# A decode step of attention and MLP on one core: K and V loaded with one key head to 32 partitions, and the softmax laid out to match

## The chip, the core and the metric

The kernel runs on one NeuronCore of one Trainium2 chip. The metric is device time in microseconds (us) of one execution; lower is better. Three runs of the kernel before gave 98.59, 98.72 and 98.76 us, so the median is 98.72 us. The profile was taken in a further execution, which took 98.62 us.

## What is computed

One token `x` of 1024 values goes through a layer norm. An attention block and an MLP work beside each other on the result, and both are added to `x`:

```python
xn = layernorm(x)
q = xn @ wq                                  # 32 query heads of 128; 4 key heads, 8 queries each
k, v = the last 4096 rows of each key head's cache
p = softmax(q k / sqrt(128));  o = p v       # per query head
A = o @ wo                                   # (1, 4096) @ (4096, 1024)
B = gelu(layernorm(xn) @ w1 + b1) @ w2 + b2  # 1024 -> 3584 -> 1024
out = x + A + B
```

Everything is bf16. Each weight and each cache row is read once: wq, wo 8.4 MB each, w1, w2 7.3 MB each, and of K and V 4.2 MB each (four key heads of 1 MB). That makes 39.86 MB from HBM for a few matrix rows of work.

## The kernel before

There is no planner: each engine's list is written out by hand, and semaphores tie the lists together. The order of the transfers is the order of SP's list, since one queue on SP issues nearly all of them.

**Transfers (SP).** wq in two pieces (L232, issued on L159), K in two (L230), w1 in one (L235). Then SP waits for turned K (L311) and loads V in two pieces into the same tile `KV` (L312). After the q projection (L313) it loads w2 in two pieces (L314) over wq's part of the tile `BIG`; after the first MLP product (`done["h"]`, L315) it loads wo in four pieces (L319) over w1's part and beyond. Line 159 is the helper's issue of every weight but wo.

**Layout of K and V.** `pairs` (L226) takes two key heads for one transfer: partition 2m+g holds 64 consecutive rows of head g, a run of 16 KB, so that each transfer of 2 MB covers all 128 partitions. Every partition holds rows of one head of each pair, and even and odd partitions hold different heads.

**Turning and scores.** VectorE turns K in 32x32 blocks of bf16, 128x4096 at a time, four times (`turn_k`, L284). q is turned the same way (L292) and spread into the zeroed tile `QBD` by four copies on VectorE and four on ScalarE (L303, L305). TensorE makes the scores in four PSUM banks: 32 matmuls of 128x512 (L467). Since two heads share the block of a turn, a first matmul per bank (L441) writes -1e30 where query and key head do not belong together.

**Softmax.** VectorE takes the maximum over 4 banks (L333) and over four groups of partitions (L337 to L342); ScalarE takes the exponential of 2048 columns (L345); VectorE turns the result into `PT` (L349). TensorE multiplies it with V in 32 matmuls (L496). The sum over partitions is a matmul with `B64` (L484); VectorE scales by the reciprocal with a mask `HALF` (L380) and adds the blocks.

**The MLP.** w1 is multiplied in 56 matmuls (L480), the gelu runs on small tiles (L358 to L371), and w2 and 16 of the 32 rows of wo go through 11 rounds of eight matmuls (L505). Each round waits for a count on `s_feed`, which GpSimd raises when transfers land (L407 to L414). The other 16 rows of wo come last (L530, L528), then two copies and the store (L401, L403).

All additions onto banks that are prepared beforehand go through one helper, so their matmuls carry its line, L424; they are told apart by their tiles.

Of the kernel before, what the change touches and what calls it, by code (L numbers as in the profile page):

```python
# [27 lines left out]
PAIRS = 2  # L28
FAR = -1e30
# [24 lines left out]
def bass_parallel_sum__sliding_block_cached__mixer_channel_mlp__decode_kernel(  # L54
# [22 lines left out]
    s_x, s_b1, s_b2, s_v, s_out = (nc.alloc_semaphore(n) for n in ("s_x", "s_b1", "s_b2", "s_v", "s_out"))  # L77
    s_w1 = sems("s_w1", len(W1_CHUNKS))
    s_wq = [nc.alloc_semaphore("s_wq")] * len(WQ_CHUNKS)
    s_k = sems("s_k", PAIRS)  # L80
# [19 lines left out]
    B64 = sb("B64", [128, 64], f32)  # L100
    HALF4 = sb("HALF4", [64, 4], f32)
    HALF = sb("HALF", [64, PAIRS], f32)
    OTHER = sb("OTHER", [2, 128], bf16)
    ALT = sb("ALT", [2, 512], bf16)
# [11 lines left out]
    QBD = sb("QBD", [128, PAIRS * 512], bf16)  # L116
    HT = sb("HT", [128, FC], f32)
    U2 = sb("U2", [128, FC], f32)
    MX2 = sb("MX2", [128, 2], f32)
    MX8 = sb("MX8", [32, 8], f32)  # L120
    MXR = sb("MXR", [32, 1], f32)
# [7 lines left out]
    REC = sb("REC", [64, 1], f32)  # L129
# [40 lines left out]
    def pool_wait():  # L170
# [15 lines left out]
    POOL.mark(pool.memset(HALF4[:, :], 1.0))  # L186
    POOL.mark(pool.memset(OTHER[:, :], FAR))
    POOL.mark(pool.memset(ALT[:, :], 0.0))
# [12 lines left out]
    POOL.mark(pool.affine_select(  # L201
        out=OTHER[:, :].rearrange("p (x g h) -> p x g h", g=2, h=REP),
        in_=OTHER[:, :].rearrange("p (x g h) -> p x g h", g=2, h=REP),
        pattern=[[0, 8], [-1, 2], [0, REP]], compare_op=ALU.not_equal, fill=0.0, base=0, channel_multiplier=1))
    POOL.mark(pool.affine_select(
        out=ALT[:, :].rearrange("p (x g) -> p x g", g=2), in_=ALT[:, :].rearrange("p (x g) -> p x g", g=2),
        pattern=[[0, 256], [-1, 2]], compare_op=ALU.not_equal, fill=1.0, base=0, channel_multiplier=1))
    POOL.mark(pool.affine_select(
        out=HALF4[:, :], in_=HALF4[:, :], pattern=[[-16, 4]], compare_op=ALU.is_ge, fill=0.0,
        base=0, channel_multiplier=1))  # L210
    pool_wait()
    POOL.mark(pool.affine_select(
        out=HALF4[:, :], in_=HALF4[:, :], pattern=[[16, 4]], compare_op=ALU.is_ge, fill=0.0,
        base=15, channel_multiplier=-1))
# [11 lines left out]
    def pairs(cache, c):  # L226
        return cache[0, 2 * c:2 * c + 2, SK - W:SK, :].rearrange("g (m i) d -> m g (i d)", m=64)

    def load_k(c):
        sp.dma_start(KV[:, c * 8192:(c + 1) * 8192], pairs(A_k_cache, c)).then_inc(s_k[c], 16)  # L230
# [9 lines left out]
    def layernorm_stats(src, n, name):  # L240
# [37 lines left out]
        out=B64[:, :].rearrange("p (k r) -> p k r", k=2),  # L278
        in_=identf[:, :].rearrange("p (q r) -> p r q", q=4).unsqueeze(1).to_broadcast([128, 2, 32, 4]),
# [12 lines left out]
    C["qtb"] = DVE.mark(dve.transpose(QTB, Q32))  # L292
# [3 lines left out]
    QD = QBD[:, :].rearrange("p (c e b h) -> p c e b h", c=PAIRS, e=4, b=4)  # L296
    QS = QTB.rearrange("p (j e c) -> p e c j", j=4, e=4)
    for b in range(4):
        for c in range(PAIRS):
            to = QD[32 * b:32 * b + 32, c, :, b, 16 * c:16 * c + 16].rearrange("p e (u j) -> p e u j", j=4)  # L300
            of = QS[32 * b:32 * b + 32, :, 4 * c:4 * c + 4, :]
            if PAIRS * b + c < 4:
                C["d_QBD"] = DVE.mark(dve.tensor_copy(to, of))  # L303
            else:
                C["a_QBD"] = ACT.mark(act.activation(out=to, in_=of, func=ACTF.Copy))  # L305
# [3 lines left out]
    V = KV[:, :]  # L309
    for c in range(PAIRS):  # L310
        sp.wait_ge(DVE.sem, C["kt", 2 * c + 1])  # L311
        sp.dma_start(V[:, c * 8192:(c + 1) * 8192], pairs(A_v_cache, c)).then_inc(s_v, 16)  # L312
    sp.wait_ge(done["q"], 8)  # L313
    load_chunks(W2, w2_p, W2_CHUNKS, D, s_w2)  # L314
    sp.wait_ge(done["h"], 7)  # L315
    c0 = 0
    for j, n in enumerate(WO_CHUNKS):
        first = (FC + c0) * D
        sp.dma_start(BIG[:, first:first + n * D], wo_flat[:, c0 * D:(c0 + n) * D]).then_inc(s_wo[j] if j else s_feed, HALF_FEED)  # L319
        c0 += n  # L320
# [9 lines left out]
    S = PS[:, 3 * 512:7 * 512]  # L330
    for n in range(2):
        dve.wait_ge(done["sc"], 3 + n)
        C["mx"] = DVE.mark(dve.tensor_reduce(  # L333
            out=MX2[:, n:n + 1], in_=S[:, 1024 * n:1024 * n + 1024], axis=AX.X, op=ALU.max))
    dve_wait()
    for b in range(4):
        DVE.mark(dve.tensor_copy(MX8[:, 2 * b:2 * b + 2], MX2[32 * b:32 * b + 32, :]))  # L337
    dve_wait()
    DVE.mark(dve.tensor_reduce(out=MXR[:, :], in_=MX8[:, :], axis=AX.X, op=ALU.max))
    dve_wait()  # L340
    for b in range(4):
        C["nmb"] = DVE.mark(dve.tensor_scalar(  # L342
            out=NMB[32 * b:32 * b + 32, :], in0=MXR[:, :], scalar1=-SCALE, scalar2=None, op0=ALU.mult))
# [14 lines left out]
    DVE.mark(dve.tensor_tensor(out=U2[:, :], in0=HT[:, :], in1=HT[:, :], op=ALU.mult))  # L358
    dve_wait()
    DVE.mark(dve.tensor_scalar(out=U2[:, :], in0=U2[:, :], scalar1=0.044715, scalar2=1.0,  # L360
                               op0=ALU.mult, op1=ALU.add))
    dve_wait()
    C["d_T"] = DVE.mark(dve.tensor_tensor(out=U2[:, :], in0=U2[:, :], in1=HT[:, :], op=ALU.mult))
# [11 lines left out]
    DVE.mark(dve.reciprocal(out=REC[:, :], in_=PS[0:64, 3 * 512:3 * 512 + 1]))  # L375
    dve_wait()
    dve.wait_ge(done["pv"], 8)
    for i in range(2):
        rows = slice(32 * i, 32 * i + 32)
        DVE.mark(dve.scalar_tensor_tensor(  # L380
            out=ONM.rearrange("p (i c d) -> p i c d", i=2, c=PAIRS)[:, i],
            in0=PS[rows, 512:1024].rearrange("p (c i d) -> p i c d", c=PAIRS, i=2)[:, i], scalar=REC[rows, 0:1],
            in1=HALF[rows, :].unsqueeze(2).to_broadcast([32, PAIRS, DH]), op0=ALU.mult, op1=ALU.mult))
    dve_wait()
    DVE.mark(dve.tensor_reduce(
        out=ON[:, :], in_=ONM.rearrange("p (g d) -> p d g", g=4), axis=AX.X, op=ALU.add))
# [30 lines left out]
    pe.reg_mov(turn, C["kt", 0])  # L417
# [39 lines left out]
    pe.wait_ge(DVE.sem, C["d_QBD"])  # L457
    K4 = KT[:, :].rearrange("p (x k) -> p x k", k=128)
    with pe.Fori(0, PAIRS) as c:
        pe.wait_ge(ACT.sem, C["a_QBD"])  # L460
        with pe.Fori(0, 2) as i:
            pe.wait_ge(DVE.sem, turn)
            pe.reg_add(turn, turn, 1)
            for n in range(2):
                for j in range(2):
                    for u in range(2):
                        last = add(PS[:, bass.ds(i * 1024 + (3 + n) * 512, 512)],  # L467
                                   QBD[:, bass.ds(c * 512 + (j * 256 + u * 128), 128)],
                                   K4[:, bass.ds(c * 64 + i * 32 + 16 * n, 16), j * 64 + 32 * u:j * 64 + 32 * u + 32])
            last.then_inc(done["sc"], 1)  # L470
        pe.reg_add(turn, turn, C["kt", 2] - C["kt", 1] - 1)
# [12 lines left out]
    pe.matmul(PS[0:64, 3 * 512:3 * 512 + 1], lhsT=B64[:, :], rhs=SUMP[:, :]).then_inc(done["tot"], 1)  # L484
    pe.wait_ge(ACT.sem, C["a_h8"])
    for c in range(4):
        last = add(turned[:, c], H8[:, c:512:4], FLIP[:, 0:7])
        if c == 0:
            pe.wait_ge(s_v, 32)
# [3 lines left out]
    V3 = V.rearrange("p (c x) -> p c x", c=PAIRS)  # L493
    with pe.Fori(0, 8) as i:
        for u in range(4):
            last = add(bank(1), PT[:, bass.ds(i * 256 + u * 64, 128)], V3[:, :, bass.ds(i * 1024 + u * 256, 256)])  # L496
        last.then_inc(done["pv"], 1)

    pe.wait_ge(DVE.sem, C["d_GT"])
    with pe.Fori(0, ROUNDS) as t:  # L500
        pe.wait_ge(s_feed, turn)
        pe.reg_add(turn, turn, 2 * HALF_FEED)
        for u in range(ROUND):
            for a in range(2):
                add(bank(7), GO[:, bass.ds(t * STEP + (LEAD + 2 * u - ROW - a), 128)],  # L505
                    BIG[:, bass.ds(t * (ROUND * D) + (u * D + a * 512), 512)])
# [8 lines left out]
    for j, n in enumerate(WO_ROWS[WO_HEAD:]):  # L515
# [6 lines left out]
        for c in range(c0, c0 + n):  # L522
            rhs = BIG[:, (FC + c) * D:(FC + c + 1) * D]
# [39 lines left out]
```

## Time and profile before

| | |
|---|---|
| median of three runs | 98.72 us |
| profiled execution | 98.62 us |
| its span on the core | 97.2 us (1.4 us lie around it) |
| read from HBM | 39.86 MB, 410 GB/s over the span |
| PE / DVE / ACT / POOL busy | 79.4 / 39.0 / 11.2 / 9.9 us |
| granted TensorE clock | 1.00 throughout |

A page of the profile shows busy time by engine, the span in 40 slices, the DMA queues, the chain of work that ended last, the costliest groups of instructions, and the transfers with the median time from issue to landing. PE is TensorE, DVE is VectorE, ACT ScalarE, POOL GpSimd; SPq is SP's list of transfers. A busy TensorE is not a TensorE at its peak. Idle time of an engine that does not set the end costs nothing. A transfer's time to landing includes the time it stands in its queue behind earlier ones; its own share is read from the landing of the one before it.

### The profile page before, as it was taken

How to read it: one execution, taken by the hardware profiler on the slowest of the kernel's cores; microseconds unless marked ns; L12 is line 12 of the kernel's file. 1: busy time of each engine (PE TensorE's matmuls, PEld its weight loads, DVE VectorE, ACT ScalarE, POOL GpSimd, SP SyncE). 2: the span in 40 equal slices, each digit the busy share in tenths (PEclk: the TensorE clock that was granted, in tenths of full speed). 3: DMA queues.
4: the chain of work that ended last, by engine and by line, in shares of the span. 5: the costliest groups of instructions: out<-in, count | busy, mean ns of one | idle time of the engine just before them, and what ended most of it. 6: DMA issues, size and time to landing. Idle time of an engine off the chain costs nothing.

```text
span 97.2 us, 1412 instructions
## 1 busy us (share of the span) xinstructions
PE 79.4 (82%) x389; PEld 33.4 (34%) x400; DVE 39.0 (40%) x54; ACT 11.2 (12%) x20; POOL 9.9 (10%) x27
## 2 busy tenths in 40 slices
PE   0000899977999999999299999899999999979982
PEld 0000134423444432343134444333334344334451
DVE  0000589840079986999945450060029000000001
ACT  0870000060000006000003500200000100000001
POOL 6999400000000000000000000000000000000000
DMA  2998888899999988889999999999899999899990
GB/s 64 651 473 378 378 378 378 378 458 432 401 431 549 590 378 378 378 378 401 415 431 431 431 492 431 431 458 394 384 475 499 458 431 431 368 389 436 388 379 3
DMA packets 1989, 39.88 MB, mean 410 GB/s; under 512 B 322, under 2 KB 324, under 8 KB 452
## 3 DMA queue, kind: packets, MB, share of 16 engines
q1 hardware_dynamic: 1876, 39.85, 95.7%
q10 hardware_dynamic: 112, 0.01, 0.1%
q8 instruction: 1, 0.02, 0.1%
HBM read 39.86 MB, written 0.00 MB: 410 GB/s over the span
## 4 chain that ended last, share of the span: by engine, by line
DMA 54%; PE 30%; DVE 11%; issue 1%; SPq 1%; ACT 1%
DMA BIG<-in_A_wo_dram 32%; PE PS L424 30%; DMA BIG<-in_A_wq_dram 22%; DVE KT L284 9%; SPq L319 1%; DVE Pb L292 1%; DVE QBD L303 1%; ACT Pb L290 1%; DVE Pb L401 0%; SPq L159 0%; PE PS L510 0%
## 5 line engine op out<-in xcount | busy, mean ns | idle before, releaser
L424 PE MATMUL PS<-BIG,GO 128*128 (+1 forms) x137 | 21.5, 334 | 1.8 <-POOLq L414 0.8
L284 DVE STREAM_TRANSPOSE KT<-KV 128x4096 bf16<-128x4096 bf16 x4 | 17.5, 4424 | 6.9 <-DMA KV<-in_A_k_cache_dram 6.9
L424 PE MATMUL PS<-BIG,XZ 128*128 x64 | 14.0, 379 | 1.3 <-DMA BIG<-in_A_wq_dram 1.3
L424 PEld LDWEIGHTS PS<-BIG,GO 128*128 (+1 forms) x148 | 9.9, 97 | 13.5 <-issue 5.9
L424 PE MATMUL PS<-BIG,YZ 128*128 x56 | 12.4, 380 | 0.1
L428 PE MATMUL PS<-QBD 128*128 128x512 bf16 x38 | 10.1, 434 | 0.4 <-POOL HALF L217 0.4
L424 PEld LDWEIGHTS PS<-BIG,XZ 128*128 x64 | 6.2, 97 | 9.0 <-issue 2.7
L424 PE MATMUL PS<-KT,QBD 128*128 x32 | 7.4, 380 | 1.9 <-DVE KT L284 1.9
L420 PE MATMUL PS<-XBRP,onesb 1*128 1x512 bf16 x2 | 1.0, 617 | 9.7 <-DMA XBRP<-in_A_x_dram 9.7
L424 PE MATMUL PS<-KV,KT 128*128 x32 | 8.3, 381 | 0.5
L401 DVE CAST Pb<-PS 64x256 bf16<-64x256 f32 x1 | 0.4, 416 | 20.0 <-PE PS L510 20.0
L424 PEld LDWEIGHTS PS<-BIG,YZ 128*128 x56 | 5.4, 96 | 7.1 <-issue 1.2
L428 PEld LDWEIGHTS PS<-QBD 128*128 128x128 bf16 x38 | 4.0, 108 | 6.9 <-issue 3.7
L242 DVE BATCH_NORM_STATS2 BN<-PS 128x6 f32<-128x512 f32 x2 | 1.3, 688 | 10.7 <-PE PS L420 10.7
L424 PEld LDWEIGHTS PS<-KT,QBD 128*128 x32 | 3.0, 97 | 6.2 <-issue 3.3
L424 PEld LDWEIGHTS PS<-KV,KT 128*128 x32 | 3.1, 96 | 5.3 <-issue 3.8
L380 DVE SCALAR_TENSOR_TENSOR QBD<-PS,REC,HALF 32x256 f32<-32x256 f32 x2 | 0.9, 474 | 6.8 <-PE PS L424 6.8
L345 ACT ACTIVATE Pb<-PS,NMB 128x2048 bf16<-128x2048 f32 x1 | 2.0, 1967 | 13.8 <-DVE NMB L342 13.8
L420 PEld LDWEIGHTS PS<-XBRP,onesb 1*128 1x128 bf16 x2 | 0.1, 108 | 9.7 <-DMA XBRP<-in_A_x_dram 9.7
L349 DVE STREAM_TRANSPOSE KT<-Pb 128x2048 bf16<-128x2048 bf16 x1 | 2.3, 2310 | 2.1 <-ACT Pb L345 2.1
L333 DVE TENSOR_REDUCE MX<-PS 128x1 f32<-128x1024 f32 x2 | 2.4, 1206 | 1.3 <-PE PS L424 1.3
L354 DVE COPY HT<-PS 128x28 f32<-128x28 f32 x1 | 0.2, 207 | 6.2 <-PE PS L424 6.2
(81 smaller groups left out, 42.1 us busy)
## 6 DMA issues: line engine op xcount, KB each, us to landing
BIG<-in_A_wq_dram SPq DMA_DIRECT2D x1, 7168.0 KB, 21.1
BIG<-in_B_w_dram SPq DMA_DIRECT2D x1, 7168.0 KB, 46.0
KV<-in_A_k_cache_dram SPq DMA_DIRECT2D x2, 2048.0 KB, 27.7
KV<-in_A_v_cache_dram SPq DMA_DIRECT2D x2, 2048.0 KB, 14.5
BIG<-in_B_w_dram SPq DMA_DIRECT2D x1, 4096.0 KB, 20.5
BIG<-in_A_wo_dram SPq DMA_DIRECT2D x1, 4096.0 KB, 23.1
BIG<-in_B_w_dram SPq DMA_DIRECT2D x1, 3072.0 KB, 27.1
BIG<-in_A_wo_dram SPq DMA_DIRECT2D x1, 2816.0 KB, 29.4
```

Of the source, the lines that this page charges most:

```text
L242: DVE.mark(dve.bn_stats(out=BN[:, 12 * n + 6 * i:12 * n + 6 * i + 6], in_=src[:, 512 * i:512 * i + 512]))
L284: C["kt", n] = DVE.mark(dve.transpose(KT[:, n * 4096:(n + 1) * 4096], KV[:, n * 4096:(n + 1) * 4096]))
L290: C["q32"] = ACT.mark(act.activation(out=Q32, in_=bank(7), func=ACTF.Copy))
L292: C["qtb"] = DVE.mark(dve.transpose(QTB, Q32))
L303: C["d_QBD"] = DVE.mark(dve.tensor_copy(to, of))
L319: sp.dma_start(BIG[:, first:first + n * D], wo_flat[:, c0 * D:(c0 + n) * D]).then_inc(s_wo[j] if j else s_feed, HALF_FEED)
L333: C["mx"] = DVE.mark(dve.tensor_reduce(out=MX2[:, n:n + 1], in_=S[:, 1024 * n:1024 * n + 1024], axis=AX.X, op=ALU.max))
L345: C["exp"] = ACT.mark(act.activation(out=Pb[:, :], in_=S, func=ACTF.Exp, bias=NMB[:, 0:1], scale=SCALE, accum_out=SUMP[:, 0:1]))
L349: C["d_pt"] = DVE.mark(dve.transpose(PT[:, 0:2048], Pb[:, :]))
L420: last = pe.matmul(bank(2 + i), lhsT=onesb[0:1, :], rhs=XB[0:1, 8 * i:8 * i + 8, :])
L424: return pe.matmul(to, lhsT=lhsT, rhs=rhs, start=False, stop=False, skip_group_check=True, **place)
L428: pe.matmul(to, lhsT=zeros[:, 0:128], rhs=zeros[:, 0:512], skip_group_check=True, **how)
```

## The change

- **Layout.** K and V are each loaded by four transfers of 1 MB. Head g goes to partitions 32g to 32g+31, each of which holds 128 consecutive rows, a run of 32 KB. K's four transfers share one semaphore, and so do V's.
- **Place of V.** V no longer goes over K, but over wq's part of `BIG`. SP issues it right after the q projection, and no longer waits for K to be turned. The second piece of w2 and the first of wo now lie in w1's part and wait for `done["h"]`; the last three pieces of wo lie over V and wait for `done["pv"]`.
- **Turning.** K, q and the exponentials are turned as 32-bit words that hold two bf16 values, so each turn has half the elements.
- **Scores.** 32 matmuls as before, into two banks instead of four. `QBD` becomes a sliding window, and no -1e30 mask is written: four matmuls with zeros take the place of the masks. GpSimd no longer builds `OTHER`, `ALT` and `HALF`, and zeroes a tile `PT` of 128x4096 (over K) once K is turned.
- **Softmax.** One maximum over 1024 columns; the maximum over groups of partitions by two 128x32 turns and a reduction; the exponential of 1024 columns; four turns of 32 partitions into `PT`. In both kernels the maximum is one value per query head; the scaling (four instructions of 32x128) needs no mask any more.
- **Gelu.** Two instructions in place of three ahead of the exponential.

The core of the diff:

```diff
-    def pairs(cache, c):
-        return cache[0, 2 * c:2 * c + 2, SK - W:SK, :].rearrange("g (m i) d -> m g (i d)", m=64)
-    def load_k(c):
-        sp.dma_start(KV[:, c * 8192:(c + 1) * 8192], pairs(A_k_cache, c)).then_inc(s_k[c], 16)
+    def load_cache(dst, cache, semaphore):
+        for g in range(HKV):
+            sp.dma_start(dst[32 * g:32 * g + 32, :], cache[0, g, SK - W:SK, :].rearrange("(m i) d -> m (i d)", m=32)).then_inc(
+                semaphore, 16)
...
     def turn_k(n):
-        dve.wait_ge(s_k[n // 2], 16)
-        C["kt", n] = DVE.mark(dve.transpose(KT[:, n * 4096:(n + 1) * 4096], KV[:, n * 4096:(n + 1) * 4096]))
+        if n == 0:
+            dve.wait_ge(s_k, 16 * HKV)
+        C["kt", n] = DVE.mark(dve.transpose(
+            KT[:, n * 4096:(n + 1) * 4096].bitcast(f32), KV[:, n * 4096:(n + 1) * 4096].bitcast(f32)))
...
-    for c in range(PAIRS):
-        sp.wait_ge(DVE.sem, C["kt", 2 * c + 1])
-        sp.dma_start(V[:, c * 8192:(c + 1) * 8192], pairs(A_v_cache, c)).then_inc(s_v, 16)
     sp.wait_ge(done["q"], 8)
-    load_chunks(W2, w2_p, W2_CHUNKS, D, s_w2)
+    load_cache(V, A_v_cache, s_v)
+    load_chunks(W2, w2_p, W2_CHUNKS[:1], D, s_w2)
     sp.wait_ge(done["h"], 7)
+    load_chunks(W2, w2_p, W2_CHUNKS[1:], D, s_w2[1:], W2_CHUNKS[0])
     for j, n in enumerate(WO_CHUNKS):
-        first = (FC + c0) * D
+        first = (c0 - TAIL if j else TAIL + FC) * D
+        if j == 1:
+            sp.wait_ge(done["pv"], 8)
...
+    pool.wait_ge(DVE.sem, C["kt", 3])
+    C["PT"] = POOL.mark(pool.memset(PT, 0.0))
...
     C["exp"] = ACT.mark(act.activation(
-        out=Pb[:, :], in_=S, func=ACTF.Exp, bias=NMB[:, 0:1], scale=SCALE, accum_out=SUMP[:, 0:1]))
+        out=Pb[:, 0:1024].rearrange("p (x s w) -> p x w s", s=32, w=2),
+        in_=S.rearrange("p (x w s) -> p x w s", s=32, w=2),
+        func=ACTF.Exp, bias=NMB[:, 0:1], scale=SCALE, accum_out=SUMP[:, 0:1]))
+    dve.wait_ge(POOL.sem, C["PT"])
     dve.wait_ge(ACT.sem, C["exp"])
-    C["d_pt"] = DVE.mark(dve.transpose(PT[:, 0:2048], Pb[:, :]))
+    for g in range(HKV):
+        rows = slice(32 * g, 32 * g + 32)
+        C["d_pt"] = DVE.mark(dve.transpose(
+            PT[rows, :].bitcast(f32).rearrange("p (x a g h) -> p x a g h", a=4, g=HKV, h=REP)[:, :, :, g, :],
+            Pb[rows, 0:1024].bitcast(f32)))
...
-        pe.matmul(PS[:, bass.ds(n * 512 + 3 * 512, 512)], lhsT=OTHER[:, :], rhs=ALT[:, :], start=True, stop=False,
+        pe.matmul(PS[:, bass.ds(n * 512 + 3 * 512, 512)], lhsT=GO[:, 0:128], rhs=GO[:, 0:512], start=True, stop=False,
...
-        for u in range(4):
-            last = add(bank(1), PT[:, bass.ds(i * 256 + u * 64, 128)], V3[:, :, bass.ds(i * 1024 + u * 256, 256)])
+        for u in range(2):
+            for w in range(2):
+                last = add(bank(1), PT[:, bass.ds(i * 512 + (u * 256 + w), 128, step=2)],
+                           V[:, bass.ds(i * 2048 + (u * 1024 + w * 512), 512)])
```

More of the change, by code (lines that the diff above doesn't have):

```diff
@@ L99, in bass_parallel_sum__sliding_block_cached__mixer_channel_mlp__decode_kernel @@
     E4 = sb("E4", [32, 4 * 128], bf16)
[L100 to L104, printed above, removed]
+    B128 = sb("B128", [128, 128], f32)
     EDGE = sb("EDGE", [2, 132], bf16)
@@ L185, in bass_parallel_sum__sliding_block_cached__mixer_channel_mlp__decode_kernel @@
     POOL.mark(pool.memset(EDGE[:, :], 0.0))
[L186 to L188 removed]
+    POOL.mark(pool.memset(MX[:, 0:32], 0.0))
     POOL.mark(pool.memset(E4[:, :], 0.0))
@@ L291, in bass_parallel_sum__sliding_block_cached__mixer_channel_mlp__decode_kernel @@
     dve.wait_ge(ACT.sem, C["q32"])
-    C["qtb"] = DVE.mark(dve.transpose(QTB, Q32))
+    C["qtb"] = DVE.mark(dve.transpose(QTB.bitcast(f32), Q32.bitcast(f32)))
     dve_wait()
@@ L295, in bass_parallel_sum__sliding_block_cached__mixer_channel_mlp__decode_kernel @@
     act.wait_ge(POOL.sem, C["consts"])
-    QD = QBD[:, :].rearrange("p (c e b h) -> p c e b h", c=PAIRS, e=4, b=4)
-    QS = QTB.rearrange("p (j e c) -> p e c j", j=4, e=4)
-    for b in range(4):
-        for c in range(PAIRS):
[L300 to L305, printed above, removed]
+    QD = QBD[:, 0:4 * QW].rearrange("p (w n e) -> p w n e", w=2, e=2)
+    QS = QTB.rearrange("p (j e c w) -> p w c j e", j=4, e=2, w=2)
+    for g in range(HKV):
+        rows = slice(32 * g, 32 * g + 32)
+        to = QD[rows, :, 24 + 32 * g:32 + 32 * g, :].rearrange("p w (u j) e -> p w u j e", j=4)
+        of = QS[rows, :, 2 * g:2 * g + 2, :, :]
+        if g < 2:
+            C["d_QBD"] = DVE.mark(dve.tensor_copy(to, of))
+        else:
+            C["a_QBD"] = ACT.mark(act.activation(out=to, in_=of, func=ACTF.Copy))
     for n in range(2, 4):
         turn_k(n)
-    V = KV[:, :]
-    for c in range(PAIRS):
-        sp.wait_ge(DVE.sem, C["kt", 2 * c + 1])
-        sp.dma_start(V[:, c * 8192:(c + 1) * 8192], pairs(A_v_cache, c)).then_inc(s_v, 16)
     sp.wait_ge(done["q"], 8)
-    load_chunks(W2, w2_p, W2_CHUNKS, D, s_w2)
+    load_cache(V, A_v_cache, s_v)
+    load_chunks(W2, w2_p, W2_CHUNKS[:1], D, s_w2)
     sp.wait_ge(done["h"], 7)
+    load_chunks(W2, w2_p, W2_CHUNKS[1:], D, s_w2[1:], W2_CHUNKS[0])
     c0 = 0
     for j, n in enumerate(WO_CHUNKS):
-        first = (FC + c0) * D
+        first = (c0 - TAIL if j else TAIL + FC) * D
+        if j == 1:
+            sp.wait_ge(done["pv"], 8)
         sp.dma_start(BIG[:, first:first + n * D], wo_flat[:, c0 * D:(c0 + n) * D]).then_inc(s_wo[j] if j else s_feed, HALF_FEED)
@@ L328, in rows_of @@
         return values.rearrange("p (r u) -> p r u", u=ROUND).unsqueeze(2).to_broadcast([128, n, 2, ROUND])
[L330 to L334, printed above, removed]
+    pool.wait_ge(DVE.sem, C["kt", 3])
+    C["PT"] = POOL.mark(pool.memset(PT, 0.0))
+    S = PS[:, 3 * 512:5 * 512]
+    dve.wait_ge(done["sc"], 4)
+    DVE.mark(dve.tensor_reduce(out=MX[:, 0:1], in_=S, axis=AX.X, op=ALU.max))
     dve_wait()
-    for b in range(4):
-        DVE.mark(dve.tensor_copy(MX8[:, 2 * b:2 * b + 2], MX2[32 * b:32 * b + 32, :]))
+    DVE.mark(dve.transpose(MX[:, 32:64], MX[:, 0:32]))
     dve_wait()
-    DVE.mark(dve.tensor_reduce(out=MXR[:, :], in_=MX8[:, :], axis=AX.X, op=ALU.max))
+    DVE.mark(dve.tensor_reduce(
+        out=MX[:, 64:96].rearrange("p (a h) -> p a h", a=4),
+        in_=MX[:, 32:64].rearrange("p (a h) -> p h a", a=4).unsqueeze(1).to_broadcast([128, 4, REP, 4]),
+        axis=AX.X, op=ALU.max))
     dve_wait()
-    for b in range(4):
-        C["nmb"] = DVE.mark(dve.tensor_scalar(
-            out=NMB[32 * b:32 * b + 32, :], in0=MXR[:, :], scalar1=-SCALE, scalar2=None, op0=ALU.mult))
+    DVE.mark(dve.transpose(MX[:, 96:128], MX[:, 64:96]))
+    dve_wait()
+    C["nmb"] = DVE.mark(dve.tensor_scalar(out=NMB[:, :], in0=MX[:, 96:97], scalar1=-SCALE, scalar2=None, op0=ALU.mult))
     act.wait_ge(DVE.sem, C["nmb"])
     C["exp"] = ACT.mark(act.activation(
-        out=Pb[:, :], in_=S, func=ACTF.Exp, bias=NMB[:, 0:1], scale=SCALE, accum_out=SUMP[:, 0:1]))
+        out=Pb[:, 0:1024].rearrange("p (x s w) -> p x w s", s=32, w=2),
+        in_=S.rearrange("p (x w s) -> p x w s", s=32, w=2),
+        func=ACTF.Exp, bias=NMB[:, 0:1], scale=SCALE, accum_out=SUMP[:, 0:1]))
+    dve.wait_ge(POOL.sem, C["PT"])
     dve.wait_ge(ACT.sem, C["exp"])
-    C["d_pt"] = DVE.mark(dve.transpose(PT[:, 0:2048], Pb[:, :]))
+    for g in range(HKV):
+        rows = slice(32 * g, 32 * g + 32)
+        C["d_pt"] = DVE.mark(dve.transpose(
+            PT[rows, :].bitcast(f32).rearrange("p (x a g h) -> p x a g h", a=4, g=HKV, h=REP)[:, :, :, g, :],
+            Pb[rows, 0:1024].bitcast(f32)))
     act.wait_ge(done["h"], 7)
@@ L357, in bass_parallel_sum__sliding_block_cached__mixer_channel_mlp__decode_kernel @@
     dve_wait()
-    DVE.mark(dve.tensor_tensor(out=U2[:, :], in0=HT[:, :], in1=HT[:, :], op=ALU.mult))
+    DVE.mark(dve.scalar_tensor_tensor(out=U2[:, :], in0=HT[:, :], scalar=0.044715, in1=HT[:, :],
+                                      op0=ALU.mult, op1=ALU.mult))
     dve_wait()
[L360 to L363, printed above, removed]
+    C["d_T"] = DVE.mark(dve.scalar_tensor_tensor(out=U2[:, :], in0=U2[:, :], scalar=1.0, in1=HT[:, :],
+                                                 op0=ALU.add, op1=ALU.mult))
     act.wait_ge(DVE.sem, C["d_T"])
@@ L374, in bass_parallel_sum__sliding_block_cached__mixer_channel_mlp__decode_kernel @@
     dve.wait_ge(done["tot"], 1)
-    DVE.mark(dve.reciprocal(out=REC[:, :], in_=PS[0:64, 3 * 512:3 * 512 + 1]))
+    DVE.mark(dve.reciprocal(out=REC[:, :], in_=PS[:, 3 * 512:3 * 512 + 1]))
     dve_wait()
     dve.wait_ge(done["pv"], 8)
[L378 to L383, printed above, removed]
+    for j in range(4):
+        DVE.mark(dve.tensor_scalar(
+            out=ONM[:, 128 * j:128 * j + 128], in0=PS[32 * j:32 * j + 32, 512 + 128 * j:512 + 128 * j + 128],
+            scalar1=REC[32 * j:32 * j + 32, 0:1], scalar2=None, op0=ALU.mult))
     dve_wait()
     DVE.mark(dve.tensor_reduce(
-        out=ON[:, :], in_=ONM.rearrange("p (g d) -> p d g", g=4), axis=AX.X, op=ALU.add))
+        out=ON[:, :], in_=ONM.rearrange("p (j d) -> p d j", j=4), axis=AX.X, op=ALU.add))
     dve_wait()
@@ L416, in bass_parallel_sum__sliding_block_cached__mixer_channel_mlp__decode_kernel @@
     turn = pe.alloc_register("turn")
-    pe.reg_mov(turn, C["kt", 0])
+    pe.reg_mov(turn, C["d_QBD"])
     pe.wait_ge(s_x, 16)
@@ L456, in bass_parallel_sum__sliding_block_cached__mixer_channel_mlp__decode_kernel @@
                   skip_group_check=True)
[L457 to L460, printed above, removed]
+    pe.wait_ge(ACT.sem, C["a_QBD"])
+    K4 = KT[:, :].rearrange("p (x a k w) -> p a x w k", a=4, k=64, w=2)
+    QE = QBD[:, 0:4 * QW].rearrange("p (w n e) -> p w e n", w=2, e=2)
+    with pe.Fori(0, 2) as n:
+        pe.wait_ge(DVE.sem, turn)
+        pe.reg_add(turn, turn, C["kt", 3] - C["d_QBD"])
         with pe.Fori(0, 2) as i:
-            pe.wait_ge(DVE.sem, turn)
-            pe.reg_add(turn, turn, 1)
-            for n in range(2):
+            for a in range(2):
                 for j in range(2):
[L466 to L469, printed above, removed]
+                    for w in range(2):
+                        last = add(PS[:, bass.ds(n * 512 + 3 * 512, 512)],
+                                   QE[:, w, j, bass.ds(i * -16 + (24 - 8 * a), 128)],
+                                   K4[:, bass.ds(i * 2 + a, 1), bass.ds(n * 16, 16), w, 32 * j:32 * j + 32])
             last.then_inc(done["sc"], 1)
-        pe.reg_add(turn, turn, C["kt", 2] - C["kt", 1] - 1)
     pe.reg_mov(turn, 2 * HALF_FEED)
@@ L488, in bass_parallel_sum__sliding_block_cached__mixer_channel_mlp__decode_kernel @@
         if c == 0:
-            pe.wait_ge(s_v, 32)
+            pe.wait_ge(s_v, 16 * HKV)
     last.then_inc(done["hT"], 1)
     pe.wait_ge(DVE.sem, C["d_pt"])
-    V3 = V.rearrange("p (c x) -> p c x", c=PAIRS)
     with pe.Fori(0, 8) as i:
-        for u in range(4):
-            last = add(bank(1), PT[:, bass.ds(i * 256 + u * 64, 128)], V3[:, :, bass.ds(i * 1024 + u * 256, 256)])
+        for u in range(2):
+            for w in range(2):
+                last = add(bank(1), PT[:, bass.ds(i * 512 + (u * 256 + w), 128, step=2)],
+                           V[:, bass.ds(i * 2048 + (u * 1024 + w * 512), 512)])
         last.then_inc(done["pv"], 1)
@@ L522, in bass_parallel_sum__sliding_block_cached__mixer_channel_mlp__decode_kernel @@
         for c in range(c0, c0 + n):
-            rhs = BIG[:, (FC + c) * D:(FC + c + 1) * D]
+            rhs = BIG[:, (c - TAIL) * D:(c - TAIL + 1) * D]
             for a in range(4):
```

45 lines of the change are left out of this document (12 added, 33 removed).

## The prediction

> **What bounds the kernel now.** I read the chain of work that ended last first, since it names what sets the end. By engine and line:
>
> ```profile
> DMA 54%; PE 30%; DVE 11%; issue 1%; SPq 1%; ACT 1%
> ```
>
> and its last pieces in order of time (start, length, what):
>
> ```profile
> 62.72 0.43 SPq L319
> 63.16 0.04 issue
> 63.20 31.34 DMA BIG<-in_A_wo_dram
> 94.53 0.04 issue
> 94.58 0.73 PE PS L424 x20
> ```
>
> The end waits for wo's third piece, issued at 63.20 us and landed at 94.53, and then for 2.7 us of work. The chain goes on to the 56 matmuls with w1 (L424) that SP waits for before it issues wo. That reading is a trap: 31.34 us for a piece of 1 MB is time in a queue. So I looked at whether the queue is ever empty: the table by stretches (PE, PEld, DVE, ACT, POOL busy, clock, DMA share, GB/s), the queues, and the transfers.
>
> ```profile
> 2.00:95.00 93.00, 78.95 (x381) 33.23 (x396) 38.59 (x53) 10.81 (x19) 8.47 (x21) 1.00 1.00 428
> ```
>
> ```profile
> q1 hardware_dynamic: 1876, 39.85, 95.7%
> ...
> BIG<-in_A_wq_dram SPq DMA_DIRECT2D x1, 7168.0 KB, 21.1
> BIG<-in_B_w_dram SPq DMA_DIRECT2D x1, 7168.0 KB, 46.0
> ...
> BIG<-in_B_w_dram SPq DMA_DIRECT2D x1, 3072.0 KB, 27.1
> ```
>
> The 16 DMA engines are at a share of 1.00 for the 93 us between 2 and 95. The kernel is bound by transfers from end to end, and the other engines fit beside them.
>
> Next, what each tensor costs the queue: issue plus time to landing gives the moment it lands, and the one before it is subtracted. The issue times are in the timeline of SP's queue, K's landings in the view of its tile:
>
> ```profile
> L230 SPq DMA_DIRECT2D KV<-in_A_k_cache_dram x2: 602/610/617, 1.7 to 2.4; - x2
> ...
> DMA to landing us min/median/max: 25.7/27.7/29.7
> ```
>
> - wq's large piece, issued at 1.27, lands 21.06 later (the chain): at 22.3.
> - K's second piece: 2.4 + 29.7 = 32.1. K took 9.8 us for 4.19 MB: 429 GB/s, in runs of 16 KB.
> - w1: 3.0 + 46.0 = 49.0, so 16.9 us for 7.34 MB: 434 GB/s, in runs of 56 KB.
> - V's second piece, issued at 47.4, lands after 11.4: 58.8, 9.8 us again.
> - w2's second piece: 48.6 + 27.1 = 75.7, 16.9 us, 434 GB/s. wo's last piece, issued at 63.7, lands after 31.5: 95.2, so 19.5 us for 8.39 MB, 430 GB/s.
>
> Every tensor moves at 429 to 434 GB/s, 27 GB/s to an engine, whatever its run length and place in HBM. Every one of these transfers also writes all 128 partitions.
>
> **The change, part by part.**
>
> *VectorE's and ScalarE's work.* Four turns of K took 4.42 us each (128x4096 bf16). With half the elements they should take 2.2 each, 8.8 us less in all. Two maxima of 1.2 us become one; the exponential goes from 2048 to 1024 columns (1.97 to about 1.1); one gelu instruction of 0.2 us goes. All this lies beside full DMA engines, and gains nothing by itself. I cost it at 0. If a 32-bit turn were no faster than 4.42 us, that would still be today's work, which is hidden.
>
> *GpSimd* loses the building of the masks (2.3 us for one instruction, L205), ahead of TensorE's idle loop: 0. It gains zeroing 128x4096: 128x1536 takes 1.38 us (L215), so 3.7 us, after K's last turn. What is queued behind it are the counts for `s_feed`, not needed before w2's landing at 68.5 (48.0 + 20.5); and the turns into `PT`, which need the exponential too. 0.
>
> *TensorE*: the same 32 + 32 matmuls, four of zeros for four of masks: 0.
>
> *The waits of SP.* V's wait for turned K goes. In its place w2's second piece waits for `done["h"]`, with wo's first piece behind it, and wo's other pieces wait for `done["pv"]`. At today's rates: K is in at 32.0, turned by 42.3 (four turns and the turn of q, which waits for the q projection at 36.5), scored from 40.5 to 48.1 (32 x 0.24 us, TensorE comes out of its bias matmuls at 40.5), so the matmuls with w1 start when w1 lands, 49.0, and end 12.45 us later at 61.5. The queue still holds V and 4.2 MB of w2 then, until 68.5. A transfer needs about 2.1 us beyond its bytes (wq's first MB, 4.5 to landing, of which 2.4 are its bytes at 434 GB/s). Slack: 68.5 - 61.5 - 2.1 = 5 us. `done["pv"]` comes at about 72, and the queue then holds work until wo's first piece lands at 85.4: slack 11 us. Both waits cost 0. If the first one ran late by more than 5 us, each further us would be one us at the end.
>
> *Eight issues for four.* Each takes 0.6 us on SP (L230). K's four follow at 1.7 to 4.2, with wq busy until 22; V's four start at 36.5, with w1 busy until 49. 0.
>
> *Runs of 32 KB for 16 KB.* At w1's 434 GB/s in place of 429, K and V take 9.67 us each for 9.8. Gain at most 0.2 us in all, and at the end, since the queue is the bound.
>
> *Where the transfers write.* Here the change touches the bound, and the trace of before has no row for it: no large transfer writes fewer than 128 partitions. Now each of the eight writes 32, and they stand in one queue behind each other, so that all 16 engines write into the same 32 partitions at a time. Two bounds. If only the engine limits (the nearest row), K and V take 9.67 us each and nothing is lost. If SBUF's ways in are spread evenly over the partitions, and 128 partitions take just the 434 GB/s that every tensor reaches, 32 take a quarter: 38.7 us each, 58 us more. I take the middle of these by ratio, a factor of 2 (two engines to each way in): 217 GB/s, 19.3 us each, 2 x (19.3 - 9.8) = 19.1 us more. I don't take the nearest row, though it says nothing is lost: that all tensors stop at one rate whatever their run length or source looks like a limit at the destination or the engine, and rows that all write 128 partitions cannot tell these two apart.
>
> [...]
>
> The whole stays covered at half rate: K in at 41.6, w1 at 58.5, matmuls with w1 done at 71; V in at 77.9, product with V done at 86.7; w2's first piece holds the queue until 87.5, wo's first until 104.5. So the 19.1 us reach the end undiminished.
>
> **Sum.** 98.62 (the profiled execution) + 19.1 = **117.7 us**. The median of the three runs is 0.1 higher, well within what I can say here.
>
> **Rivals.**
>
> 1. *The engines are the limit, not the place they write to.* For it: every row of the trace, at 27 GB/s to an engine. Against it: only that one rate for all tensors looks like a limit at the destination just as well. Then the sum is 98.62 - 0.2 = 98.4 us, not slower than before; it decides if 1 MB into 32 partitions takes 2.4 us like any other MB. It is also the outcome if the runs are cut and rearranged on their way so that the engines spread anyway (98.6).
> 2. *The engines share unevenly.* Of two engines at one way in, the first goes ahead, and later writes to other partitions than the second. They collide only until they are one or two transfers apart, and the loss is between one transfer's time twice over (2 x 2.4 = 4.8 us) and three quarters of the full 19: 103.4 to 113 us. For it: the queue is deep and engines need not wait for one another. Against: with even turns two engines stay level.
> 3. *A quarter of the rate*, the other bound: 98.62 + 58 = 156 us.
> 4. *A new wait starves the queue.* It needs `done["h"]` later than 66.4 at today's rates, 5 us after what I work out, and costs one us per us: 99 to 101. The matmuls with w1 cannot start before w1 lands, but nothing I see holds them longer.
>
> **Chances.** Half rate 0.60; rival 1 0.22; rival 2 0.11; rival 3 0.05; rival 4 0.02. A measurement of this kernel tells a difference from none beyond about 0.2% (0.2 us). Rival 1 lies on that edge, so I split it: 0.10 faster, 0.12 the same. Slower: 0.60 + 0.11 + 0.05 + 0.02 = 0.78. The likeliest case's own range is 114 to 119.5 us (207 to 240 GB/s); alone it leaves out 4 in 10, so the range reaches down to rival 1: 98.3 to 119.5, and leaves out rival 3 alone.
>
> **What would show it.** In the stretch after wq's landing at 22 us the table should show some 217 GB/s at a DMA share near 1.00 until 41.6; K's last piece should land then, w1 at 58.5, V at 77.9. The matmuls with w1 should wait for w1, and nothing in the list of waits should show SP late. If K lands at 32, rival 1 holds and I am wrong by all of the 19 us; if it lands near 37 with engines out of step, rival 2. A stretch of DMA share well under 1.00 between 60 and 70 would be rival 4. The turns should show 2.2 us each, and it should not matter.

## The result, and the profile after

The changed kernel takes 121.97 us (median of six runs, 121.02 to 122.52), the kernel before 98.72 (six runs, 98.59 to 98.80): a ratio of 1.2324, 95% interval 1.2273 to 1.2376. It is slower, as forecast, but by 23.3 us instead of 19.1, and so 2.5 us above the range.

The profiled execution took 122.05 us. From its page, the span, the granted TensorE clock and the share of the DMA engines in 40 slices, and the chain of work that ended last:

```profile
span 120.3 us, 1412 instructions
...
PEclk9999999999999975559999999955899999955899
DMA  3999797999889977979789998899899999989940
...
PE 9%; DVE 0%; issue 0%
```

Two things differ from before: the clock drops to a half three times, where it was full throughout, and the chain ends in TensorE's work and no longer goes back to a transfer (it can be followed back only to 107.08 us, hence its 9%). The DMA engines, however, are as full as they were. What they move while K and V are loaded is seen in the table by stretches (PE, PEld, DVE, ACT, POOL busy, clock, DMA share, GB/s), here from the landing of wq to that of K and from w1's to V's:

```profile
22.90:43.00 20.10, 17.22 (x82) 7.65 (x82) 0.00 (x0) 0.60 (x1) 0.00 (x0) 1.00 1.02 229
```

```profile
60.40:80.30 19.90, 12.74 (x59) 5.87 (x59) 3.47 (x7) 2.02 (x3) 0.00 (x0) 0.94 0.99 214
```

A share of 1.02 beside 229 GB/s says that the engines are hardly ever idle, and that each packet takes twice as long (the trace has 2.56 us for a packet of 32 KB here, median from 24 to 41 us, and 1.22 from 97 to 104 us, where wo's first piece goes to all 128 partitions in packets of the same size): the queue is not starved, its packets are slow. (The GB/s of a stretch are rough at its ends; landings are not.) Time that each tensor takes at the queue, from landing to landing as in the prediction, and the start of the two last copies, with the experiments told below:

| us | wq lands | K takes | w1 takes | V takes | last of wo lands | copies start |
|---|---|---|---|---|---|---|
| before | 22.3 | 9.8 | 17.0 | 9.7 | 95.2 | 95.5 |
| after | 22.9 | 20.1 | 17.4 | 20.0 | 116.8 | 118.7 |
| e1_wide | 22.3 | 9.9 | 16.9 | 9.7 | 95.4 | 95.7 |
| e4_half | 22.9 | 20.3 | 17.2 | 20.0 | 116.8 | 119.0 |
| e6_stride | 22.3 | 10.1 | 16.9 | 9.7 | 95.6 | 96.0 |
| e7_short | 22.3 | 10.0 | 16.9 | 9.9 | 95.7 | 96.1 |
| e2_wide_k | 22.3 | 9.8 | 17.6 | 19.9 | 106.1 | 107.1 |
| e3_wide_v | 23.0 | 20.2 | 16.9 | 9.7 | 106.3 | 106.7 |
| e5_order | 22.6 | 19.9 | 17.1 | 19.8 | 115.9 | 116.9 |

So of 23.4 us between the two profiled executions, 10.3 come with K, 10.3 with V, 1.1 with the tensors around them; 1.5 lie between the last landing and the copies; and 0.3 lie outside the span (1.7 us after, 1.4 before). Each is rounded by itself.

The end of the chain in order of time (start, length, what), and from the list of waits the two longest of TensorE's waits after V began to load (total, times, longest):

```profile
107.08 0.22 issue
107.30 11.22 PE PS L405 x90
118.52 0.13 PE PS L491 x4
```

```profile
PE PS L405 <- DMA BIG<-in_A_v_cache_dram: 6.4, 1, 6.4
...
PE PS L405 <- POOLq L395: 4.1, 1, 4.1
```

In the changed kernel L405 is the helper that all additions go through, and L395 GpSimd's count of wo's first piece. TensorE waits 6.4 us for V and then, after seven rounds with w2, 4.1 us for wo's first piece, which landed at 107.0. It then needs 11.2 us for what lands within 9.8 us (107.0 to 116.8), at half the clock until 112 us, and the copies start 1.8 us behind the last landing. The clock, by stretches:

```profile
102.00:104.00 2.00, 1.23 (x6) 0.38 (x4) 0.00 (x0) 0.00 (x0) 0.00 (x0) 1.00 1.18 508
104.00:106.00 2.00, 0.00 (x0) 0.00 (x0) 0.00 (x0) 0.00 (x0) 0.00 (x0) 0.84 0.91 391
106.00:108.00 2.00, 0.70 (x2) 0.36 (x3) 0.00 (x0) 0.00 (x0) 0.00 (x0) 0.50 0.97 417
108.00:110.00 2.00, 2.00 (x6) 0.74 (x5) 0.00 (x0) 0.00 (x0) 0.00 (x0) 0.50 0.92 394
110.00:112.00 2.00, 2.00 (x7) 0.62 (x5) 0.00 (x0) 0.00 (x0) 0.00 (x0) 0.50 1.16 496
112.00:114.00 2.00, 2.00 (x10) 0.90 (x9) 0.00 (x0) 0.00 (x0) 0.00 (x0) 0.96 0.79 330
```

The turns do what they were meant to:

```profile
L257 DVE STREAM_TRANSPOSE KT<-KV 128x2048 f32<-128x2048 f32 x4 | 9.0, 2290 | 21.9 <-DMA KV<-in_A_k_cache_dram 21.9
```

2.29 us for each, half of the 4.42 before, and it is worth nothing: VectorE waits 21.9 us for K.

### The profile page after: what moved, and what is told of

It is laid out like the page before. It is cut to its first block, busy times and chain, and to the rows that moved or that the text cites. A ratio compares the mean times of both kernels' runs of the same rounds, so it can differ in the third digit from the quotient of the medians.

```text
span 120.3 us, 1412 instructions
## 1 busy us (share of the span) xinstructions
PE 85.3 (71%) x400; PEld 36.2 (30%) x400; DVE 29.5 (25%) x50; ACT 10.1 (8%) x18; POOL 9.6 (8%) x21
## 5 line engine op out<-in xcount | busy, mean ns | idle before, releaser
L405 PE MATMUL PS<-BIG,GO 128*128 (+1 forms) x148 | 24.1, 356 | 4.6 <-POOLq L395 4.1
L405 PEld LDWEIGHTS PS<-BIG,GO 128*128 (+1 forms) x148 | 10.6, 101 | 18.3 <-issue 11.7
L405 PE MATMUL PS<-KT,QBD 128*128 x32 | 9.5, 466 | 9.1 <-ACT QBD L279 9.1
L405 PE MATMUL PS<-BIG,XZ 128*128 x64 | 14.0, 379 | 1.0 <-DMA BIG<-in_A_wq_dram 1.0
L257 DVE STREAM_TRANSPOSE KT<-KV 128x2048 f32<-128x2048 f32 x4 | 9.0, 2290 | 21.9 <-DMA KV<-in_A_k_cache_dram 21.9
L405 PE MATMUL PS<-BIG,YZ 128*128 x56 | 12.4, 380 | 1.9 <-DMA BIG<-in_B_w_dram 1.9
L409 PE MATMUL PS<-QBD 128*128 128x512 bf16 x38 | 11.2, 470 | 0.0
L405 PE MATMUL PS<-BIG,KV 128*128 x32 | 9.1, 456 | 0.1
L405 PEld LDWEIGHTS PS<-BIG,XZ 128*128 x64 | 6.2, 98 | 8.8 <-issue 2.4
L405 PEld LDWEIGHTS PS<-KT,QBD 128*128 x32 | 3.6, 114 | 14.9 <-issue 12.7
L405 PEld LDWEIGHTS PS<-BIG,YZ 128*128 x56 | 5.4, 96 | 8.9 <-issue 3.1
L305 POOL MEMSET KV<- 128x4096 bf16 x1 | 3.5, 3516 | 45.9 <-DVE KT L257 45.9
L405 PE MATMUL PS<-FLIP,H 8*128 8x7 bf16 x4 | 0.4, 180 | 6.9 <-DMA BIG<-in_A_v_cache_dram 6.4
L405 PEld LDWEIGHTS PS<-BIG,KV 128*128 x32 | 3.6, 114 | 5.1 <-issue 2.5
L362 DVE TENSOR_SCALAR QBD<-PS,REC 32x128 f32<-32x128 f32 x4 | 1.4, 345 | 7.5 <-PE PS L405 7.4
L331 DVE STREAM_TRANSPOSE KV<-Pb 32x512 f32<-32x512 f32 x4 | 2.8, 702 | 1.7 <-ACT Pb L322 1.6
```

Source lines behind the costliest of these rows:

```text
L305: C["PT"] = POOL.mark(pool.memset(PT, 0.0))
L331: C["d_pt"] = DVE.mark(dve.transpose(PT[rows, :].bitcast(f32).rearrange("p (x a g h) -> p x a g h", a=4, g=HKV, h=REP)[:, :, :, g, :], Pb[ ...
L362: DVE.mark(dve.tensor_scalar(out=ONM[:, 128 * j:128 * j + 128], in0=PS[32 * j:32 * j + 32, 512 + 128 * j:512 + 128 * j + 128], scalar1=REC ...
L405: return pe.matmul(to, lhsT=lhsT, rhs=rhs, start=False, stop=False, skip_group_check=True, **place)
L409: pe.matmul(to, lhsT=zeros[:, 0:128], rhs=zeros[:, 0:512], skip_group_check=True, **how)
```

## The experiments

**My theory**: engines that write into the same 32 partitions at a time hold each other up. (That they share ways into SBUF is an assumption; what the trace shows is K's 20.1 us for the 9.8 before.) Its rivals: the runs of 32 KB or their place in HBM, the number of transfers, the number of partitions in a transfer, engines that share unevenly. Four kernels change only the transfers of K and V (in each, K's and V's; but for the transfers and the counts that wait for them, every engine runs the same instructions as in the changed kernel).

**e1_wide**: one transfer over all 128 partitions, still runs of 32 KB.

```diff
-        for g in range(HKV):
-            sp.dma_start(dst[32 * g:32 * g + 32, :], cache[0, g, SK - W:SK, :].rearrange("(m i) d -> m (i d)", m=32))...
+        sp.dma_start(dst, cache[0, :, SK - W:SK, :].rearrange("g (m i) d -> m g (i d)", m=32)).then_inc(semaphore, 16)
...
```

> The changed kernel, but K and V are each loaded by one transfer over all 128 partitions (head g on partitions 4m+g), still in runs of 32 KB; the heads are therefore mixed in the scores and the result is not the reference's, with the same instructions on every engine. If the place (32 partitions at a time) costs the time, K and V take 9.7 us each again and the kernel 98.4 us, the rest of the change being worth nothing. If runs of 32 KB or the way they lie in HBM cost it, it stays near 122 us.

Measured: 99.1 us (eight runs, 99.03 to 99.28), ratio to before 1.0036 (1.0024 to 1.0049). K's one transfer, in the view of its tile:

```profile
L201 SPq DMA_DIRECT2D KV<-in_A_k_cache_dram x1: 611/611/611, 1.7 to 1.7; - x1
...
DMA to landing us min/median/max: 30.5/30.5/30.5
```

It lands at 32.1, 9.9 us after wq, and the end is 23 us earlier than the changed kernel's. Neither the runs of 32 KB nor their place in HBM cost anything, nor does anything else in the change cost more than 0.4 us. They gain nothing either: I expected 98.4.

**e4_half**: two transfers of 64 partitions.

```diff
-        for g in range(HKV):
-            sp.dma_start(dst[32 * g:32 * g + 32, :], ...
+        for h in range(2):
+            sp.dma_start(dst[64 * h:64 * h + 64, :], cache[0, 2 * h:2 * h + 2, SK - W:SK, :].rearrange(
+                "g (m i) d -> m g (i d)", m=32)).then_inc(semaphore, 16)
...
```

> As the changed kernel, but K and V each in two transfers of 64 partitions (two heads interleaved on each half), runs of 32 KB; heads mixed, so not the reference's result. If the rate goes with the number of partitions written (half at 32, full at 64), K and V take 9.7 us and the kernel 98.5. If partitions 0 to 63 lead to the same ways in as 0 to 31, K still takes about 20 us and the kernel about 122.

Measured: 121.85 us (two runs, 121.25 and 122.45). The same stretch as above:

```profile
22.90:43.00 20.10, 18.91 (x82) 8.09 (x82) 0.00 (x0) 0.60 (x1) 0.00 (x0) 0.92 1.02 229
```

Twice as many partitions, and not a byte more per us. So the rate does not go with the number of partitions: K's 4.19 MB take 20.3 us here, 207 GB/s, and 20.1 us in the changed kernel, 209 GB/s.

**e6_stride**: four transfers of 32 partitions, every fourth one.

```diff
-            sp.dma_start(dst[32 * g:32 * g + 32, :], ...
+            sp.dma_start(dst[g:128:4, :], ...
```

> As the changed kernel, four transfers of 32 partitions each for K and for V, but every fourth partition (g, g+4, ..., g+124) instead of 32 in a row; heads mixed, so not the reference's result. If it is the number of partitions, or the eight transfers of 1 MB, it stays at 122 us. If it is which partitions are written, it comes down: to 98.5 if the engines then each have a way in of their own, between 98.5 and 122 if some still share.

Measured: 99.3 us (three runs, 99.22 to 99.40), ratio 1.0054 (1.0037 to 1.0072). K's four transfers:

```profile
L202 SPq DMA_DIRECT2D KV<-in_A_k_cache_dram x4: 517/590/686, 1.6 to 3.6; - x4
...
DMA to landing us min/median/max: 23.3/26.1/28.9
```

The last lands at 32.4, 10.1 us after wq; the kernel is 0.8 us over the 98.5 that I expected. As many transfers of as many partitions as in the changed kernel, in the same runs, and the rate is full again (4.19 MB in 10.1 us, 415 GB/s): it is which partitions are written together. That every fourth partition gives the whole rate is more than I could tell beforehand; how the rows of a transfer are dealt to the engines isn't seen in the trace.

**e7_short**: four transfers of 1 MB, each over 128 partitions in runs of 8 KB.

```diff
-            sp.dma_start(dst[32 * g:32 * g + 32, :], cache[0, g, SK - W:SK, :].rearrange("(m i) d -> m (i d)", m=32))...
+            sp.dma_start(dst[:, 4096 * g:4096 * g + 4096], cache[0, g, SK - W:SK, :].rearrange("(m i) d -> m (i d)", m=128))...
```

> As the changed kernel, four transfers of 1 MB for K and for V, but each over all 128 partitions in runs of 8 KB; heads and rows mixed, so not the reference's result. If eight transfers of 1 MB are what costs, 122 us. If the place costs, 98.6 to 99.0 (runs of 8 KB a little slower than 32 KB).

Measured: 99.54 us (99.51 and 99.56), 0.5 us over the top of what I expected. Beside e1_wide, eight transfers instead of two cost some 0.4 us, runs of 8 KB included (K takes 10.0 us, V 9.9).

**e2_wide_k and e3_wide_v**: one of the two tensors loaded as in e1_wide, the other as in the changed kernel.

> The changed kernel with K alone in one transfer over 128 partitions, V in four transfers of 32 (K's heads mixed, so not the reference's result). If the two losses at the queue are alike and add, K takes 9.7 us and the last piece of wo lands some 10.5 us earlier than in the changed kernel, near 106.4; the kernel takes 109 to 111.5 us, depending on how cold TensorE comes to its last rounds.

> The changed kernel with V alone in one transfer over 128 partitions, K in four transfers of 32 (V's heads mixed, so not the reference's result). Last piece of wo 10.5 us earlier than in the changed kernel, near 106.4. V lands at 70 us while the product with w1 runs until 73, so TensorE does not wait for V, comes later to its rounds with w2 and idles less before the last rounds: 108.5 to 109.5 us, the end right behind the last landing if the idle stretch is what costs the last 1.5 us.

Measured: 110.57 us with wide K (110.56 and 110.58), 110.03 with wide V (109.95 and 110.09). Beside e1_wide the last landing is 10.7 us later with V alone narrow (106.1 - 95.4), 11.0 with K alone, and 21.5 with both in the changed kernel: the losses add. The second expectation was 0.5 us low at its top end; its other half held. With wide V the copies start 0.4 us behind the last landing and the kernel is the faster one, although its last landing is the later one; with wide K, where TensorE waits for V, they start 1.0 us behind it.

**e5_order**: heads 0, 2, 1, 3.

```diff
-        for g in range(HKV):
+        for g in (0, 2, 1, 3):
```

> The changed kernel with the four transfers of K and of V in the order of heads 0, 2, 1, 3 (the result is the reference's). If engines that share a way in go level, the order changes nothing: 122 us. If some run ahead by a transfer, the collisions would go where neighbours in the queue write different halves: 103 to 117.

Measured: 120.21 us (120.10 and 120.32), 1.1 us under the 121.29 that the changed kernel took in other runs (e12_again, below), of which 0.8 lie in the last landing. K and V take 19.9 and 19.8 us, 0.2 less each. Were engines a transfer ahead of others, far more should have gone; that the little comes from the borders between transfers is my reading.

**e8_warm**: idle matmuls where TensorE waits for wo's first piece, which splits the loop of rounds in two.

```diff
...
+    rounds(0, FC // ROUND)
+    with pe.Fori(0, 9):
+        for i in range(2):
+            pe.matmul(bank(5), lhsT=identb[:, :], rhs=XZ[:, 0:512], start=True, stop=True, skip_group_check=True)
+    rounds(FC // ROUND, ROUNDS)
```

> The changed kernel with 18 idle matmuls (4.0 us) put between TensorE's seventh and eighth round, where it waits for wo's first piece at half the clock afterwards; the result is the reference's. If the halved clock of the last rounds is what puts the end 1.8 us behind the last landing, the granted clock stays 1.00 there and the time falls by 1.0 to 1.6 us, to about 120.6. If the landings alone set the end, nothing changes.

Measured: 121.52 us (four runs, 121.44 to 122.14). The miss is instructive. TensorE stays busy, and its pace is near that of the full clock: the last four rounds and the 40 matmuls behind them take 8.91 us, and 8.4 in e9_ahead, below, at a clock of 1.00 (107.3 to 115.7 us). The timeline of TensorE:

```profile
102.89 4.05 PE L493 MATMUL PS<-XZ,identb 128*128 128x512 bf16 x18
107.05 8.91 PE L405 MATMUL PS<-BIG,GO 128*128 x72
117.18 0.73 PE L405 MATMUL PS<-BIG,GO 128*32 128x256 bf16 x20 [1.22 <-DMA BIG<-in_A_wo_dram]
```

The copies now start 0.4 us behind the last landing, but that landing is at 117.8 in place of 116.8. In the changed kernel wo's second piece follows the first by 6.7 us (107.0 to 113.7), here by 7.9 (106.8 to 114.6). The queues between 110 and 113 us show what came in between (packets, MB, share):

```profile
q1 hardware_dynamic: 87, 1.26, 99.9%
q8 instruction: 1, 0.02, 2.2%
```

One packet of instructions, 16 KB: 2.2% of 16 engines over 3 us is 1.06 us of one engine. In the changed kernel that packet goes between 115 and 118 us, when the data are all but there. With the loop written twice TensorE's program is longer, and the packet comes earlier, amid wo; that it holds TensorE's instructions I take from this, the trace doesn't say. That it delays wo by its 1.1 us fits in place and size; it is inferred, not tried apart.

**e9_ahead and e12_again**: the same matmuls ahead of the first round, with the loop written once; and the changed kernel again on the same chip.

```diff
     pe.wait_ge(DVE.sem, C["d_GT"])
+    with pe.Fori(0, 9):
+        for i in range(2):
+            pe.matmul(bank(5), lhsT=identb[:, :], rhs=XZ[:, 0:512], start=True, stop=True, skip_group_check=True)
```

> The changed kernel with the same 18 idle matmuls (4.0 us) put ahead of the first round with w2 instead of between the seventh and the eighth, so that TensorE comes to the wait for wo's first piece without an idle stretch and with only a few instructions more in its program; the result is the reference's. If the halved clock after idling puts the end behind the last landing, the clock is 1.00 in the last 12 us, the copies start within 0.5 us of the last landing, and the time is 1 to 1.5 us below the changed kernel's on the same chip. If the time follows the landings alone, no difference.

> The changed kernel once more, beside the other on the same chip: 121 to 122.5 us as before. If the idle stretch sets the spread, runs with a lower mean clock are the longer ones, by about 1.5 us between clocks of 0.87 and 0.91.

Measured: 120.59 us (five runs, 120.46 to 120.82) against 121.29 (six runs, 121.03 to 121.87). The end of the chain in e9_ahead:

```profile
89.54 26.48 DMA BIG<-in_A_wo_dram
116.03 0.04 issue
116.07 0.73 PE PS L405 x19
116.80 0.20 PE PS L494 x4
```

The chain goes back to wo again; the last landing is at 116.7, the copies start 0.4 us later, and the clock is full from 96 us on, as TensorE now waits for wo's first piece for 1.7 us in place of 4.1. In e12_again the last landing is at 116.8 and the copies start 1.0 us later. 0.7 us less by idle work alone: the halved clock is what puts the end behind the landings. The gain is smaller than I wrote, since the changed kernel loses only 0.6 us there in this execution (1.0 less the 0.4 of the kernel before), against 1.5 in the first. The clock, first a stretch of e9_ahead, then e12_again:

```profile
108.00:110.00 2.00, 1.85 (x9) 0.84 (x9) 0.00 (x0) 0.00 (x0) 0.00 (x0) 1.00 0.84 360
```

```profile
104.00:106.00 2.00, 0.00 (x0) 0.00 (x0) 0.00 (x0) 0.00 (x0) 0.00 (x0) 1.00 0.95 409
106.00:108.00 2.00, 0.76 (x2) 0.35 (x3) 0.00 (x0) 0.00 (x0) 0.00 (x0) 0.74 0.89 383
108.00:110.00 2.00, 1.78 (x5) 0.73 (x5) 0.00 (x0) 0.00 (x0) 0.00 (x0) 0.50 1.05 451
110.00:112.00 2.00, 1.95 (x8) 0.83 (x8) 0.00 (x0) 0.00 (x0) 0.00 (x0) 0.91 1.05 451
```

In e12_again it is low for 3.4 us (1.04 in the second of its stretches, 2.0 and 0.36), in the first execution for 6.8 (0.64, 6.0 and 0.16), after the same wait of 4.1 us. Why it is twice as long in one, no run here shows. The other executions fall in line. The copies start 0.4 us behind the last landing where the clock is 1.00 (in the mean before and in e1_wide, e6_stride and e7_short, from 96 us on in e9_ahead), and also in e3_wide_v and e8_warm; 1.0 us in e12_again, where it is low for 3.4 us after that wait, in e2_wide_k, where after such a wait (4.07 us) the weight loads come every 0.43 us from 96.9 to 99.8 and then every 0.21, and in e5_order (mean clock 0.914); 1.8 us in the changed kernel's first execution, where it is low for 6.8, and 2.3 in e4_half, which has the lowest mean, 0.873. The kernel's spread goes the same way: the runs at mean clocks of 0.87 took 121.87 and 122.52 us, those at 0.90 to 0.92 took 121.02 to 122.05. Clock and time do not go strictly together, though: 121.08 and 121.53 were both at about 0.915.

**e10_masks and e11_gelu3**: e1_wide with GpSimd's masks, built as in the kernel before and not used; and e1_wide with the gelu in three instructions.

> The kernel with K and V over all 128 partitions (e1_wide), and GpSimd builds the masks again that nothing uses. e1_wide has 1.70 us outside its span, the kernel before 1.38. If GpSimd's shorter list accounts for that, it falls to 1.4; otherwise it stays at 1.7, and the time at 99.1.

> e1_wide with the gelu in three instructions as before. If the two fused instructions account for the 0.33 us outside the span, it falls to 1.4 and the time to 98.8; otherwise 1.7 and 99.1.

Measured: 99.16 us (eight runs, 99.04 to 99.47) and 99.25 (eight runs, 99.10 to 99.88), outside the span 1.66 and 1.74 us (medians; e1_wide 1.72, the kernel before 1.38 to 1.41). Neither the masks nor the gelu account for the 0.3 us outside the span.

## Why the prediction was right, and where it was wrong

- **What bounds the kernel**: right. The DMA engines set the end before, and in every kernel here the copies start within 0.4 to 2.3 us of the last landing.
- **Where the transfers write**: that the place costs the time is shown. Full rate returns when the same bytes in the same runs go to all 128 partitions (e1_wide, K in 9.9 us) or to every fourth (e6_stride, 10.1), and stays at a half with 64 in a row (e4_half, 20.3). The ways into SBUF that one of my two bounds argues with were an assumption; no run shows them. The factor was chosen as the middle of the two, and no row of before would have given it; by the rows alone it was luck that it came so near. It turned out to be 2.06: 40.1 us for K and V, 209 GB/s for the 217 I took. **Mis-sized: 20.6 us for 19.1** (2 x (19.3 - 9.8) as written is 19.0).
- **What I left out: the neighbours.** wq lands 0.5 us later and w1 takes 0.4 longer. wq lands at 22.3 to 22.4 us in all kernels where the next transfer runs at full rate, every fourth partition included, and at 22.6 to 23.0 in the table where it is a slow one. Engines that are done earlier begin the slow transfer, and collide with the others' tail: this is my reading, the trace doesn't name the engines. 1.1 us in all.
- **The step that failed: "So the 19.1 us reach the end undiminished", and 0 for TensorE.** I followed the transfers' delay to the end and checked that no wait starved the queue, which held. I did not ask what the engines do while they wait. TensorE, which used to come to its rounds with w2 late, now waits for V, then catches up, idles 4.1 us and begins its last rounds at half the clock: 1.5 us more in the profiled execution, 0.6 in that of e12_again; e9_ahead took 0.7 back with idle work. The prediction's own times held that stretch: w2's first piece at 87.5 and wo's first at 104.5, with seven rounds of 12.9 us in all between them, leave TensorE idle for some 4 us.
- **Outside the span**: 0.3 us that I had at 0. It is in every kernel made from the changed one (medians of 1.66 to 1.80 us against 1.38 to 1.41), the wide ones included. Which part of the change does it stays open; the masks and the gelu do not.
- Together: 1.5 + 1.1 + 1.5 + 0.3 = 4.4 us, 122.05 - 117.7. The range's top allowed for a rate of 207 GB/s, which covers what K and V took: by them alone it would have been 98.6 + 20.6 = 119.2 us. It held nothing for the other 2.9 us.
- **Rival 1**: refuted as stated. Its own sum was off as well: with K and V wide the kernel takes 99.1 and not 98.4, since runs of 32 KB gain nothing (K 9.9 us for 9.7) and 0.3 us come outside the span. **Rival 2**: its 103 to 113 us lie well under what was measured, and e5_order moved K and V by 0.2 us each, which fits engines that stay level. **Rival 3**: refuted. **Rival 4**: SP waits for `done["h"]` until 73.2 us, and the queue then holds V until 80.3 and w2's first piece until 90.0. It never ran dry.
- **Half the elements in a turn** (2.29 us for the 2.2 expected), the shorter exponential and the fewer instructions: worth nothing, as forecast; e1_wide has them all, and it is 0.4 us slower than the kernel before.

No version here beats the kernel before.

## What to carry to other kernels

Ask of each transfer not only how long its runs are but which partitions it writes at a time: here 32 or 64 in a row got half the rate (209 and 207 GB/s), and 32 spread over the 128, every fourth one, all of it (415). A DMA share of 1.02 beside some 209 GB/s by the landings, for 429 before, is how this looked. And when a transfer gets slower, look at what idles meanwhile: here TensorE's last rounds began at a clock of 0.50 after 4.1 us of waiting (the changed kernel), and at 1.00 after 1.7 (e9_ahead).

## What the runs showed of the hardware that I had not expected

- 32 partitions at a distance of four took 4.19 MB in 10.1 us (e6_stride, 415 GB/s), 64 in a row needed 20.3 us (e4_half, 207 GB/s).
- A packet of 16 KB of instructions took 1.1 us of one of the 16 DMA engines (2.2% and 2.3% of 16 over 3 us, e8_warm and the changed kernel). With a longer program it came between 110 and 113 us in place of 115.9, amid wo, and the landing behind it was 1.1 us later (e8_warm); that one caused the other is inferred.
- After the same idle stretch of 4.1 us TensorE's clock stayed at a half for 3.4 us in one execution (e12_again) and for 6.8 in another (the changed kernel's first).
- wq landed at 22.6 to 23.0 us where a transfer to 32 or 64 partitions in a row followed it in the queue, at 22.3 to 22.4 where one at full rate did; w1 took 17.1 to 17.6 us and 16.9 to 17.0.
